# Loading two bias rows in eight one-row loads in place of five, in an adaLN attention and MLP decode kernel

## The chip, the core and the metric

The kernel runs on one core of a Trainium2 chip. The core has TensorE (PE, matmuls and their weight loads, PEld), VectorE (DVE), ScalarE (ACT), GpSimd (POOL) and SyncE (SP). SP, ACT and POOL also issue the transfers between device memory and the on-chip memory, which 16 DMA engines carry out. The metric is the device time of one execution in microseconds (us), the median of several runs. Lower is better.

## What is computed

A decode step for 8 sequences of one token each, in f32, all sizes as in the reference:

```python
x = A_x                                               # 8 x 1 x 512
mod = (silu(c) @ w_mod).reshape(8, 6, 1, 512)         # sa, ca, ga, sb, cb, gb
h = layernorm(x) * (1 + ca) + sa
# attention: 32 query heads, 8 key/value heads, head size 128, the last 2048 of 8192 cached positions
q = h @ wq
p = softmax(einsum(q, k_window) * 128 ** -0.5)
x = x + ga * (einsum(p, v_window) @ wo)
h = layernorm(x) * (1 + cb) + sb
# dense MLP with squared ReLU, inner size 1792
r = maximum(h @ w1 + b1, 0)
x = x + gb * ((r * r) @ w2 + b2)
```

The cache windows of K and V are 67 MB each; the weights wq, wo, w1, w2 and w_mod come to another 30 MB.

## The kernel before

All large inputs pass once through an on-chip tile called `home`, which is cut into four big slots of 4 MB and a small one. A list `loads` holds the order of the large transfers: w_mod, wq, then for each of 8 key/value heads two K loads and two V loads of 4 MB each, the pieces of wo in between (two of 2 MB less some rows, with the rest gathered through POOL, and two of 2 MB), and at the end the last wo piece (L146), w1 (L134, one load of 3.5 MB) and w2 (L134, four loads of 2 MB, 1 MB and twice 256 KB). `pump` issues the next load of the list on SP's queue as soon as its slot is free, and `done` frees a slot after the last reader of its contents.

The main loop (L588 on) goes over 32 quarters of K, with V five steps behind. DVE turns K around in 128 transposes (L229), PE forms the scores (L400), `soft_a` to `soft_g` do the softmax of a head in pieces between the transposes (the last of them is the transpose of the probabilities, pT, L466), and PE forms the weighted sums of V (L486). `gather` and `project_o` (L538) multiply by wo. The order of the instructions of each engine is written out by hand: the whole kernel stands in a manual schedule.

After the loop comes the tail: the attention result is brought into rows (L648 to L652), the second norm is computed (L657 to L674), the first MLP product is summed in PSUM with b1 as the first term (L679, then L688 with w1), ReLU and square follow on DVE (L695 to L700), the second product is summed with b2 as the first term (L703, then L707 with w2), and two DVE operations (L715, L716) and one store (L717, on SP's queue) end it. `spin` stands for matmuls whose result isn't used (L581).

`late_tiles` is called once, at the step after the last head's scores (`g == HKV`, `i == 1`), right after `soft_g`. It takes the buffer that held the last head's probabilities before their transpose (`pr4`), and so its writes have to wait for that transpose (L466). It clears a part of it on POOL and loads b1 (1792 values as 4 rows of 448) and b2 (512 values as 4 rows of 128) into 4 partitions each. These loads are issued by ACT (L574).

Two things about semaphores are needed to follow the steps. Every load and store that SP or ACT issues signals its landing on one of eight load semaphores, numbered 0 to 7 here, which are handed out in turn over both queues. An instruction that depends on a load waits for its semaphore, and a load itself isn't issued before the load that had the same semaphore last has landed. And after the store, SP waits for all the semaphores of the program one after the other (L749), up to two in one instruction, before the engines meet for the end.

Of the kernel before, what the change touches and what calls it, by code (L numbers as in the profile page):

```python
# [20 lines left out]
def tile_adaln_cached_attention_mlp(  # L21
# [23 lines left out]
    NQ = D // P  # L45
# [518 lines left out]
    def late_tiles():  # L564

        late = work.tile([P, NJ, 8, 4], F32, name="pr4", bufs=1).rearrange("p j x w -> p (j x w)")
        rT = late[:, : FC * 32].rearrange("p (c b) -> p c b", b=32)
        b1_in, b2_in, x1, h2T = late[:NQ, 512 : 512 + FG], late[:NQ, 1024:1152], late[:, 1152:1280], late[:, 1280:1408]
        h2T = h2T.rearrange("p (c b) -> p c b", b=32)
        nc.gpsimd.memset(rT, 0.0)  # L570
        for t, v, cuts in ((b1_in, b1, (0, 2, 3, 4)), (b2_in, b2, (0, 2, 4))):
            v = v.rearrange("(g n) -> g n", g=NQ)
            for x, y in zip(cuts, cuts[1:]):
                nc.scalar.dma_start(t[x:y], v[x:y])  # L574
        return rT, b1_in, b2_in, x1, h2T
# [12 lines left out]
    for s in range(N + PV_LAG + 1):  # L588
        g, i = divmod(s, C)
        q, h = divmod(s, 2)  # L590
        v = s - PV_LAG
# [24 lines left out]
        if i == 1 and soft:  # L616
            soft_g(g - 1)
            if g == HKV:
                spin(2)
                rT, b1_in, b2_in, x1, h2T = late_tiles()  # L620
# [133 lines left out]
```

## Time and profile before

| | |
|---|---|
| median of 3 runs | 392.83 us (392.76 to 392.84) |
| the profiled execution's own time | 392.84 us |
| its span, first to last instruction | 391.1 us |
| mean granted TensorE clock | 0.891 of full speed |
| moved by DMA | 165.04 MB, mean 422 GB/s |
| busy: PE, DVE, ACT, POOL | 68%, 57%, 12%, 3% of the span |
| SP's queue q1 | 98.0% of the 16 DMA engines' time |
| ACT's queue q10 | 80 packets, 0.04 MB |

Times in the rows are microseconds from the start of the span. In a timeline row the first number is the start, the second the duration, then engine, line, operation and tiles; a queue's name ends in q (SPq, ACTq). In the rows that count transfers, "DMA packets" gives the packets that began in a window of time and how many of them were small, and a row such as "q1 hardware_dynamic" gives one queue's packets, megabytes and the time that its packets took as a share of the window on all 16 engines; a packet whose time goes beyond a short window makes a share above 100%. A row "A <- B: t, n, m" says that A waited for B for t us in total, n times, m us the longest.

### The profile page before, as it was taken

How to read it: one execution, taken by the hardware profiler on the slowest of the kernel's cores; microseconds unless marked ns; L12 is line 12 of the kernel's file. 1: busy time of each engine (PE TensorE's matmuls, PEld its weight loads, DVE VectorE, ACT ScalarE, POOL GpSimd, SP SyncE). 2: the span in 40 equal slices, each digit the busy share in tenths (PEclk: the TensorE clock that was granted, in tenths of full speed). 3: DMA queues.
4: the chain of work that ended last, by engine and by line, in shares of the span. 5: the costliest groups of instructions: out<-in, count | busy, mean ns of one | idle time of the engine just before them, and what ended most of it. 6: DMA issues, size and time to landing. Idle time of an engine off the chain costs nothing.

```text
span 391.1 us, 4847 instructions
## 1 busy us (share of the span) xinstructions
PE 264.5 (68%) x2078; PEld 84.7 (22%) x2078; DVE 224.2 (57%) x316; ACT 46.7 (12%) x91; POOL 10.2 (3%) x36
## 2 busy tenths in 40 slices
PE   0054958878337973798289737783788237998985
PEld 0021211112011321243013212320222011334433
DVE  1054099879057935775569457381788057855232
ACT  0020011221003100310031003100201003004010
POOL 4000000000000000030000000200000000000000
PEclk9998789989859995999599959987799859999999
DMA  8999999999999999999999999999999999999995
GB/s 328 433 429 430 441 439 436 427 432 411 432 429 432 431 432 436 431 434 422 424 431 442 434 429 419 427 432 434 429 427 422 439 432 431 421 429 428 443 409 213
DMA packets 6725, 165.04 MB, mean 422 GB/s; under 512 B 968, under 2 KB 1136, under 8 KB 1392
## 3 DMA queue, kind: packets, MB, share of 16 engines
q1 hardware_dynamic: 6336, 164.17, 98.0%
q0 software_dynamic: 288, 0.53, 0.4%
q8 instruction: 16, 0.26, 0.3%
q10 hardware_dynamic: 80, 0.04, 0.0%
q14 instruction: 5, 0.04, 0.0%
HBM read 166.24 MB, written 0.07 MB: 425 GB/s over the span
## 4 chain that ended last, share of the span: by engine, by line
DMA 56%; DVE 22%; PE 16%; issue 4%; SPq 0%; ACT 0%; DVEq 0%; ACTq 0%
DMA home<-in_A_k_cache_dram 36%; DVE kT L229 12%; DMA home<-in_A_wq_dram 9%; PE s_ps L400 5%; DMA home<-in_A_v_cache_dram 5%; DMA home<-in_B_w_dram 5%; DVE pT L466 4%; PE p_ps L431 3%; PE o_ps L486 3%; PE m_ps L345 3%; DVE pr L459 2%; DVE mx L414 1%; DVE qbd L363 1%; PE m_ps L416 1%; PE m_ps L436 1%
## 5 line engine op out<-in xcount | busy, mean ns | idle before, releaser
L229 DVE STREAM_TRANSPOSE kT<-home 128x1024 f32<-128x1024 f32 x128 | 151.6, 1221 | 78.7 <-DMA home<-in_A_k_cache_dram 71.5
L400 PE MATMUL s_ps<-kT,qst 128*32 128x512 f32 x512 | 129.4, 1076 | 11.2 <-DVE kT L229 11.2
L486 PE MATMUL o_ps<-home,pT 128*32 128x256 f32 x1024 | 68.8, 390 | 9.0 <-DVE pT L466 8.6
L486 PEld LDWEIGHTS o_ps<-home,pT 128*32 128x32 f32 x1024 | 33.9, 116 | 100.4 <-issue 59.8
L416 PE MATMUL m_ps<-ident,mx 128*1 128x128 f32 x16 | 4.3, 364 | 63.7 <-DVE mx L414 63.7
L400 PEld LDWEIGHTS s_ps<-kT,qst 128*32 128x32 f32 x512 | 14.3, 114 | 29.4 <-DVE kT L229 21.1
L466 DVE STREAM_TRANSPOSE pT<-pr 128x2048 f32<-128x2048 f32 x8 | 18.2, 2279 | 1.0 <-ACT pr L449 1.0
L443 ACT ACTIVATE pr<-p_ps,nm 128x512 f32<-128x512 f32 x8 | 5.5, 688 | 103.7 <-DVE nm L440 103.7
L449 ACT ACTIVATE pr<-pr,own 128x512 f32<-128x512 f32 x16 | 17.8, 1223 | 0.3
L416 PEld LDWEIGHTS m_ps<-ident,mx 128*1 128x1 f32 x16 | 0.7, 81 | 68.9 <-DVE mx L414 68.9
L410 ACT COPY ss<-s_ps 128x512 f32<-128x512 f32 x8 | 4.7, 585 | 89.1 <-issue 61.3
L388 ACT COPY qst<-q_ps 32x128 f32<-32x128 f32 x32 | 8.2, 256 | 52.6 <-PE q_ps L377 52.4
L263 PE MATMUL m_ps<-xsum,sel 128*128 128x1 f32 x2 | 0.6, 363 | 20.2 <-DVE xsum L261 20.2
L431 PE MATMUL p_ps<-ss,perm 128*128 128x512 f32 x16 | 13.8, 960 | 0.0
L345 PE MATMUL m_ps<-home,oX 128*32 128x512 f32 x64 | 9.8, 780 | 5.3 <-DMA home<-in_A_wq_dram 5.3
L440 DVE TENSOR_SCALAR nm<-m_ps 128x1 f32<-128x1 f32 x8 | 1.3, 158 | 18.5 <-PE m_ps L436 18.5
L363 DVE COPY qbd<-m_ps 32x128 f32<-32x128 f32 x8 | 3.0, 374 | 14.4 <-PE m_ps L360 14.3
L152 POOL MEMSET home<- 128x2048 f32 x2 | 3.6, 1803 | 240.8 <-PE wo_ps L538 240.8
L503 DVE TENSOR_SCALAR o_sb<-o_ps,bit 128x128 f32<-128x128 f32 x16 | 5.2, 328 | 7.9 <-PE o_ps L486 7.7
L459 DVE TENSOR_SCALAR pr<-pr,own 128x512 f32<-128x512 f32 x16 | 9.3, 663 | 0.8 <-ACT pr L443 0.8
L581 PE MATMUL q_ps<-ident 128*128 128x512 f32 (+1 forms) x20 | 9.6, 586 | 0.0
L241 DVE TENSOR_SCALAR e_sb<-e_sb 128x128 f32<-128x128 f32 x1 | 0.2, 227 | 15.7 <-ACT e_sb L240 15.7
(133 smaller groups left out, 149.0 us busy)
## 6 DMA issues: line engine op xcount, KB each, us to landing
home<-in_A_k_cache_dram SPq DMA_DIRECT2D x16, 4096.0 KB, 27.3
home<-in_A_v_cache_dram SPq DMA_DIRECT2D x16, 4096.0 KB, 20.2
home<-in_w_mod_dram SPq DMA_DIRECT2D x1, 6144.0 KB, 17.7
home<-in_A_wo_dram SPq DMA_DIRECT2D x2, 2048.0 KB, 24.5
home<-in_A_wo_dram SPq DMA_DIRECT2D x2, 1792.0 KB
home<-in_B_w_dram SPq DMA_DIRECT2D x1, 3584.0 KB, 23.3
home<-in_B_w_dram SPq DMA_DIRECT2D x1, 2048.0 KB, 18.2
home<-in_B_w_dram SPq DMA_DIRECT2D x1, 1024.0 KB
```

The costliest lines, as they stand in the source:

```text
L229: nc.vector.transpose(KTS[q, j][:, rows], k[:, rows, 32 * j : 32 * j + 32])
L345: nc.tensor.matmul(pqs[r][32 * g : 32 * g + 32, :], hT[:, kc, :], w[:, 4 * r + g, :], start=(kc == 0), stop=(kc == NQ - 1),)
L363: nc.vector.tensor_copy(qbd[b, 4 * r : 4 * r + 4, j].rearrange("p g (b t) -> p t g b", t=REP), pT_[b].rearrange("p (t g b) -> p t g b", t= ...
L388: nc.scalar.copy(own[b, :, :, i, 0], pq[b, :P].rearrange("p (c m t) -> p c m t", c=2, t=REP))
L400: nc.tensor.matmul(s_ps[0][32 * g : 32 * g + 32, :], qst[hk % 2][:, P * (4 * c + u) + 32 * j :][:, :32], kT[:, u], start=(c == 0 and j == ...
L416: nc.tensor.matmul(MX_[hk][0:1, :P], mx, ident, start=True, stop=True)
L431: nc.tensor.matmul(sp, perm, SS_.pop(hk), start=True, stop=True)
L449: nc.scalar.mul(X_[hk][..., w], pr, own[:, w : w + 1])
L459: nc.vector.tensor_scalar(X_[hk][..., w], pr, own[:, w : w + 1], None, op0=ALU.mult)
L466: nc.vector.transpose(PT_[hk].rearrange("p e j r -> p j e r"), X_.pop(hk).rearrange("p j x w -> p j (x w)"))
L486: nc.tensor.matmul(O_[n][32 * g : 32 * g + 32, : 2 * DH], PT_[hk][:, e, j : j + 2].rearrange("p j r -> p (j r)"), vt[:, j : j + 2, :].rear ...
L581: nc.tensor.matmul(spin_ps, ident, ident[:, None, :w].to_broadcast([P, 4, w]), start=True, stop=True)
```

## The change

Each of the two bias rows is cut at every partition, so that every one of the 4 + 4 rows is a load of its own: eight loads in place of three and two. Nothing else in the program text differs. The loads are still issued by ACT in the same place and move the same bytes. Since the semaphores are handed out in turn, three more loads also move each later load of the turn, and the store, on by three places.

```diff
@@ -568,7 +568,7 @@
         b1_in, b2_in, x1, h2T = late[:NQ, 512 : 512 + FG], late[:NQ, 1024:1152], late[:, 1152:1280], late[:, 1280:1408]
         h2T = h2T.rearrange("p (c b) -> p c b", b=32)
         nc.gpsimd.memset(rT, 0.0)
-        for t, v, cuts in ((b1_in, b1, (0, 2, 3, 4)), (b2_in, b2, (0, 2, 4))):
+        for t, v, cuts in ((b1_in, b1, range(NQ + 1)), (b2_in, b2, range(NQ + 1))):
             v = v.rearrange("(g n) -> g n", g=NQ)
             for x, y in zip(cuts, cuts[1:]):
                 nc.scalar.dma_start(t[x:y], v[x:y])
```

## The prediction

> **What bounds the kernel now.** I read the page first, then the chain that ended last, then the queues of SP and ACT, then the transfers in narrow windows of time. The page says that the transfer engines never rest before the end, and that one queue, q1, which SP feeds, is nearly all of it:
>
> ```profile
> span 391.1 us, 4847 instructions
> DMA  8999999999999999999999999999999999999995
> q1 hardware_dynamic: 6336, 164.17, 98.0%
> DMA 56%; DVE 22%; PE 16%; issue 4%; SPq 0%; ACT 0%; DVEq 0%; ACTq 0%
> ```
>
> So the last byte of w2 sets the end, and a change of the order of issue costs time where a ring (one of the 16 engines' share of q1) runs out of work. The end of the chain, in order of time (start, duration), shows the place:
>
> ```profile
> 344.11 21.05 DMA home<-in_A_v_cache_dram
> 365.19 0.05 issue
> 365.24 0.33 SPq L134
> 365.67 20.29 DMA home<-in_B_w_dram
> 386.01 1.75 PE m_ps L707 x48
> 387.78 0.30 DVE y L715
> 388.10 0.29 DVE y L716
> ```
>
> The last V load lands at 365.19, w2 follows, PE takes its last pieces as they land, and two short DVE steps and the store close the program. Next, what SP and ACT issue around the bias loads (timeline rows, one row of SP's waits, one size row with the time to landing):
>
> ```profile
> 345.59 0.33 SPq L146 DMA_DIRECT2D home<-in_A_wo_dram  x1
> 355.31 0.33 SPq L134 DMA_DIRECT2D home<-in_B_w_dram  x1
> 365.24 0.33 SPq L134 DMA_DIRECT2D home<-in_B_w_dram  x1
> SPq L134 <- DMA home<-in_A_v_cache_dram: 18.8, 2, 9.5
> 357.38 1.46 ACTq L574 DMA_DIRECT2D pr<-in_B_b_dram  x5
> 374.32 0.37 ACT L649 COPY at_i<-wo_ps 128x256 f32<-128x256 f32 x1 [17.81 <-DVE at_i L648]
> home<-in_A_wo_dram SPq DMA_DIRECT2D x1, 2048.0 KB, 24.5
> ```
>
> SP is held twice, 18.8 us in all, by V loads in front of w1 (355.31) and of the first w2 piece (365.24), although neither overwrites what those V loads bring. That is the turn of the eight semaphores: a load isn't issued before the load eight places ahead of it in the turn has landed.
>
> **The turn, before and after.** Counted through the program, the last V load has semaphore 0, the bias loads 1 to 5, the last wo load 6, w1 7, the four w2 pieces 0 to 3, the store 4. Hence w1 waits for the V load before the last, the first w2 piece for the last one: the two waits above. With eight bias loads in the same place they take 1 to 7 and 0. The wo load then gets semaphore 1, w1 gets 2, the w2 pieces 3 to 6, the store 7. So the wo load waits for the first bias row, w1 for the second, the w2 pieces for the third to sixth, the store for the seventh. The bias loads can't be issued before 357.38, because their tile is free only after the last pT transpose; the wo load was issued at 345.59. This is the part of the change that costs: SP stands still with the wo load, w1 and all of w2 behind it.
>
> **When the first bias row is in.** The queue of the bias loads is q10. Its rows, for 360.6 to 362.5, for 362.5 to 362.7, for 360 to 365 and for 365 to 370:
>
> ```profile
> q10 hardware_dynamic: 3, 0.00, 0.5%
> q10 hardware_dynamic: 1, 0.00, 0.3%
> q10 hardware_dynamic: 10, 0.01, 0.5%
> q10 hardware_dynamic: 6, 0.00, 0.1%
> ```
>
> Five loads with eight rows make 16 packets, two for each row: its bytes and its semaphore write. The first load has two rows, so its four packets are the four up to 362.7: bytes, bytes, a semaphore write by 362.5, the second one between 362.5 and 362.7. The row that becomes the first load alone is done at one of these; I take the later, 362.63 within that window, because that is when the load that comes first in the queue is known to be complete. From the last semaphore packet of a transfer to SP's next issue is 0.59 (364.65 for the last V load, shown below, to 365.24). The wo load is then issued at 362.63 + 0.59 = 363.22, 17.6 us later than now.
>
> The Trainium skill, page "DMA: Bandwidth & Descriptors", section "Why a DMA increments its semaphore by 16 and not by 1", states that a copy runs on as many engines as divide its rows, the lowest-numbered ones. By that rule, which speaks against the change, all eight rows lie on the one engine that holds the single-row loads today, and the later end is the right one; with the earlier end, at 362.00, the sum would be 0.63 us smaller, 393.1. The two packets for each row agree with it; which engine takes them no row here names.
>
> **When the rings run out.** Packet counts of 362.3 to 364.1, of 364.1 to 364.7, of 362.73 to 362.76 and of 364.64 to 364.66:
>
> ```profile
> DMA packets 30, 0.59 MB, mean 329 GB/s; under 512 B 6, under 2 KB 8, under 8 KB 8
> DMA packets 31, 0.26 MB, mean 441 GB/s; under 512 B 13, under 2 KB 15, under 8 KB 15
> DMA packets 2, 0.02 MB, mean 546 GB/s; under 512 B 1, under 2 KB 1, under 8 KB 1
> DMA packets 2, 0.02 MB, mean 819 GB/s; under 512 B 1, under 2 KB 1, under 8 KB 1
> ```
>
> Packets under 512 B are semaphore writes, and one comes when a ring ends the V load. Without q10's (two and one), 4 of 16 rings end it before 364.1 and 12 from 364.1 to 364.66. Today each goes on with a 16 KB wo packet at once, as the third and fourth rows show. After the change a ring that ends before the wo load's packets exist stands idle. How long an issue takes to its first packet on idle rings, by the two such issues of the trace (the store, window 388.42 to 389.28; w_mod at the start, window 1.7 to 1.8):
>
> ```profile
> 388.42 0.35 SPq L717 DMA_DIRECT2D out_dram<-y  x1
> DMA packets 1, 0.00 MB, mean 1 GB/s; under 512 B 0, under 2 KB 1, under 8 KB 1
> 0.74 0.39 SPq L164 DMA_DIRECT2D home<-in_w_mod_dram  x1
> DMA packets 5, 0.25 MB, mean 2458 GB/s; under 512 B 0, under 2 KB 0, under 8 KB 0
> ```
>
> That is 0.85 for the store and 1.01 for w_mod: wo packets from 364.07 to 364.23, I take 364.15, the middle, as the case is a load like the one and late in the program like the other. The 12 rings that end last hardly notice. The earlier ones lose up to 1.75 us, and for a ring that is ahead of the others this is free as long as it stays ahead.
>
> One is not. The ring that ends V at 362.74 is 1.9 ahead of the last (364.65), but spends it: rows of 369.76 to 369.78, 370.82 to 370.84, and a normal w1 packet at 376.83 to 376.85, then the count of 377.4 to 378.1:
>
> ```profile
> q8 instruction: 1, 0.02, 337.8%
> q1 hardware_dynamic: 1, 0.03, 486.2%
> q1 hardware_dynamic: 1, 0.03, 332.8%
> DMA packets 32, 0.28 MB, mean 398 GB/s; under 512 B 15, under 2 KB 15, under 8 KB 15
> ```
>
> A share times its window of 0.02 us times 16 engines is a packet's time: 1.08 for the instruction packet, 1.56 for the slow w1 packet behind it, 1.065 for a normal one. The ring does eight wo packets of 0.61 from 362.75, two of w1 from 367.65 to 369.77, the instructions, the slow one at 370.83 and five more: 370.83 + 1.56 + 5 x 1.065 = 377.71. Fifteen rings end w1 within 377.4 to 378.1, the last at 378.05. So its lead has shrunk to 0.34. Idle from 362.74 to 364.15, 1.41 us, it comes in last, 1.41 - 0.34 = 1.07 us behind the time at which w1 ends now; w2 queues behind on the same ring. With the two latencies as bounds: 0.99 to 1.15. The first ring (362.41) is 1.6 ahead at the end of w1 (that is the sixteenth, which ends before 377.4), so its 1.74 stays within the pack.
>
> **What hides nothing and what does.** w1 lands 1.07 later, L688 starts 1.07 later, w2's last piece too, and the 8 matmuls, two DVE steps and the store follow it as they do now: the 1.07 is all on the path.
> - w1 and w2 on SP wait for the second to sixth row. Ten packets at one per 0.6 to 1.2 us behind 362.63 put the sixth before 375; the wo load alone keeps the rings busy for 8 x 0.61 = 4.9 us, w1 for 8.5 more, to 377.6. Nothing runs dry; if that cover were gone, each us late is a us.
> - wo landed at 345.59 + 24.5 = 370.09; some 0.3 later is before L538 needs it (371.87 below).
> - ACT issues three more loads at 1.46 / 5 = 0.29 each, 0.9 us. Two go out once their V loads, long landed, are seen; the last one waits for the last V load, 365.19. ACT has nothing to do before 374.32, so this costs nothing; without the gap it would be 365.5 - 358.8 = 6.7 us.
> - The last b2 row is needed by L703 at 381.85, 16 us after its issue; the five loads now take from 357.38 to before 370, under 13 us.
>
> ```profile
> 371.87 1.92 PE L538 MATMUL wo_ps<-home,oT 128*32 128x512 f32 x16 [0.44 <-DVE oT L527]
> 381.85 0.48 PE L703 MATMUL m_ps<-pr,qsel 4*128 4x128 f32 x2
> ```
>
> - The close. SP's waits at the end, the four that pass from the landing of the store on, and how long SP waited for it:
>
> ```profile
> L749 SPq EVENT_SEMAPHORE  x4: 28/28/28, 390.0 to 390.2; - x4
> SPq L749 <- DMA out_dram<-y: 1.0, 1, 1.0
> ```
>
> The store's own wait is the first of four that lie 0.06 apart. With the last semaphore it is the last of them: three waits less behind the landing, -0.18 us. Bounds: 0, if the closing order follows the turn too, and -0.18.
>
> **Sum.** 1.07 - 0.18 = +0.89 on the profiled execution's 392.84 (span 391.1 and 1.74 around it): 393.73. It lies 0.01 above the median of 392.83. I predict 393.7. A measurement of this kernel tells about 0.2%, 0.79 us, from no change, so the forecast is slower by a little more than that.
>
> **Rivals.**
> - *Only the close counts* (not slower). If the three extra loads take their turn elsewhere, behind the wo load for example, the wo load keeps semaphore 6 and waits for a V load that has landed before 345.59; no ring runs dry, and 0.18 is won: 392.65. Place: the issue of L146. It decides when that issue stays before about 361.8, one latency ahead of the first ring's end. For it: the turn follows the order in which the program was laid out, which the profile doesn't show. Against: five bias loads stand ahead of the wo load now, as the two V waits of SP prove. Chance 0.28.
> - *Held, but absorbed.* The wo load is late, yet the ring at 362.74 isn't burdened again, because the instruction packet goes elsewhere or the slow packet (0.49 more) doesn't recur: the loss falls to between 0 and 0.6, and the time is 392.7 to 393.2. Against: the same program fetches the same instructions. Chance 0.11.
> - *One V packet later.* The first bias row misses its place and waits for one more V packet, (365.19 - 355.31) / 8 = 1.24 us. Then every ring stands idle, the last one 0.7, and the ring at 362.74 loses 2.65 - 0.34: 392.84 + 2.31 - 0.18 = 395.0. For it: the two rows of the first load end 0.6 apart already. Against: nothing that SP does ahead of 357.38 changes. Chance 0.11.
> - *Faster by more than 0.2%* needs 0.79 us off the transfers. The close gives 0.18; a ring relieved of a few packets of q10 gains tenths at most. Chance 0.02.
>
> **Numbers.** The forecast has 0.48; its own range is 393.3 to 394.2 (latency bounds, 0.1 either way, and some tenths for refilling the rings and for the phase of the bias row). I put 0.07 of it below 393.62. Slower by over 0.2%: 0.41 + 0.11 = 0.52. Within: 0.07 + 0.28 + 0.11 = 0.46. Faster: 0.02. The range 392.6 to 394.5 leaves out the late packet, the faster case and little else.
>
> **What would show it.** In the new profile: the wo load (L146) issued near 363.2 instead of 345.59, w1 near 364.7 instead of 355.31; SP's longest waits in front of L146 on the bias loads; fewer bytes moved from 362.4 to 364.2; w1 landing some 1 us later, L688 and L707 with it; the store's wait with no waits on loads behind it. An L146 issue that stays at 345.6 makes the prediction wrong at its first step; an issue at 363 with an unchanged end of w1, at the step of the ring that has no lead left.

## The result, and the profile after

The kernel takes 394.9 us (median of 6 runs, 394.33 to 395.21), the kernel before 392.79 beside it (392.69 to 392.95): a ratio of 1.0052, with an interval of 1.0039 to 1.0065. It is slower, as forecast, but by 2.1 us where 0.9 was forecast, and it lies outside the range of 392.6 to 394.5.

The profiled execution took 395.21, 2.37 more than the one before. From its page the span, the DMA engines' busy tenths and SP's queue:

```profile
span 393.4 us, 4851 instructions
DMA  8999999999999999999999999999999999999993
q1 hardware_dynamic: 6336, 164.17, 97.5%
```

q1's share fell from 98.0 to 97.5%, and the DMA engines rest a little earlier at the end (3 in place of 5 in the last slice), so something behind the transfers has grown longer. The end of the chain (start, duration) says where both lie:

```profile
357.51 0.23 ACTq L574
...
357.79 6.55 DMA pr<-in_B_b_dram
...
364.39 16.23 DMA home<-in_B_w_dram
...
380.66 4.61 PE m_ps L688 x32
...
387.00 3.31 PE m_ps L707 x112
390.33 0.30 DVE y L715
390.66 0.29 DVE y L716
```

It now runs through a bias row of 1,792 bytes. Behind w1's landing at 380.62 it waits for no transfer any more: L688, some short DVE steps, then all 112 matmuls of L707 in one piece. Before, PE waited for w2's pieces and had 48 matmuls of L707 left when the last ones came. What SP and ACT issue, and what SP waits for (timeline rows and rows of SP's waits):

```profile
362.89 0.33 SPq L146 DMA_DIRECT2D home<-in_A_wo_dram  x1
364.39 3.43 SPq L134 DMA_DIRECT2D home<-in_B_w_dram  x5
390.98 0.35 SPq L717 DMA_DIRECT2D out_dram<-y  x1
357.51 7.81 ACTq L574 DMA_DIRECT2D pr<-in_B_b_dram  x8
SPq L146 <- DMA pr<-in_B_b_dram: 18.3, 1, 18.3
```

The wo load was issued at 362.89 (forecast 363.22), w1 at 364.39 (364.7), and the wo load waited 18.3 us for a bias row. The turn of the semaphores works as counted. The loss is in what the rings did with a load that came this late. Packets of 363.8 to 366, first after, then before:

```profile
DMA packets 54, 0.58 MB, mean 261 GB/s; under 512 B 16, under 2 KB 19, under 8 KB 19
q1 hardware_dynamic: 47, 0.57, 88.4%
```

```profile
DMA packets 71, 0.82 MB, mean 374 GB/s; under 512 B 17, under 2 KB 21, under 8 KB 21
q1 hardware_dynamic: 63, 0.82, 87.6%
```

The share of time in q1's packets is the same, but 30% less was moved in it. The packets themselves took longer. Three rows of after (windows 364.01 to 364.03, 365.52 to 365.54, and 364.3 to 364.65), then two of before (363.615 to 363.625, and 364.3 to 364.65):

```profile
q1 hardware_dynamic: 2, 0.02, 507.5%
q1 hardware_dynamic: 1, 0.02, 475.3%
q1 hardware_dynamic: 10, 0.10, 110.9%
```

```profile
q1 hardware_dynamic: 1, 0.02, 381.9%
q1 hardware_dynamic: 13, 0.11, 77.9%
```

Share times window times 16: a first wo packet at 364.02 took 1.62 us and one at 365.53 took 1.52, where a packet of the same 16 KB took 0.61 before. In the stretch in which most rings end V (the last V load), six such packets (0.10 MB) took 1.109 x 0.35 x 16 = 6.2 us, 1.04 each, against 4.36 us for seven, 0.62 each. The end of w1 carries the mark: semaphore writes of q1 (the packets under 512 B) in the windows 377.85 to 378.8 and 379.8 to 380.3,

```profile
DMA packets 34, 0.35 MB, mean 371 GB/s; under 512 B 14, under 2 KB 14, under 8 KB 14
DMA packets 13, 0.18 MB, mean 360 GB/s; under 512 B 2, under 2 KB 2, under 8 KB 2
```

so 14 rings end w1 0.4 to 0.7 later than fifteen did before (377.4 to 378.1), and two come in more than a microsecond behind them, at 379.84 and 380.23. In the trace each packet of a ring starts within 0.01 us of the end of the one before it. Followed in this way, the first of the two is the ring whose first wo packet began at 364.02, the second the one that began at 365.53, and the same two are last at the end of w2 (388.5 and 388.8). The very last semaphore write of w2 lies in the window 388.8 to 388.9 of after and 386.7 to 386.8 of before; the row is the same for both:

```profile
DMA packets 1, 0.00 MB, mean 0 GB/s; under 512 B 1, under 2 KB 1, under 8 KB 1
```

The transfers end 2.1 us later. But y (L715) starts 390.33 - 387.78 = 2.55 later, and the other 0.5 is PE's. Its first matmuls on w1, with the granted clock of two stretches (the number behind the count), after and then before:

```profile
380.66 4.55 PE L688 MATMUL m_ps<-home,pr 128*32 128x448 f32 x32 [1.85 <-DMA home<-in_B_w_dram]
378.00:380.00 2.00, 0.81 (x4) 1.00 0.94 403
380.00:382.00 2.00, 1.34 (x8) 0.50 0.99 426
382.00:384.00 2.00, 2.00 (x20) 0.65 0.96 406
```

```profile
378.70 3.21 PE L688 MATMUL m_ps<-home,pr 128*32 128x448 f32 x32 [0.25 <-DMA home<-in_B_w_dram]
380.00:382.00 2.00, 2.00 (x24) 1.00 1.07 455
```

PE stood idle for 1.85 us in front of L688 in place of 0.25, the clock was at 0.50 from 380 to 382, and the 32 matmuls took 1.34 us longer. That used up the slack PE had against w2 and 0.5 more. Last, the waits behind the store (SP's semaphore waits in the windows 391.3 to 391.8 and 392.4 to 392.7):

```profile
L749 SPq EVENT_SEMAPHORE  x6: 17/28/28, 391.4 to 391.7; - x6
L749 SPq EVENT_SEMAPHORE  x1: 28/28/28, 392.5 to 392.5; - x1
```

Six waits now pass while the store is under way and one is left at its landing, where four were. The store was issued 390.98 - 388.42 = 2.56 later and the execution took 2.37 longer, so the close gave 0.19.

### The profile page after: what moved, and what is told of

Same layout as the page of the kernel before. It is cut to its first block, busy times and chain, and to the rows that moved or that the text cites. A ratio compares the mean times of both kernels' runs of the same rounds, so it can differ in the third digit from the quotient of the medians.

```text
span 393.4 us, 4851 instructions
## 1 busy us (share of the span) xinstructions
PE 261.3 (66%) x2078; PEld 83.2 (21%) x2078; DVE 224.0 (57%) x316; ACT 46.8 (12%) x91; POOL 10.2 (3%) x36
## 3 DMA queue, kind: packets, MB, share of 16 engines
q1 hardware_dynamic: 6336, 164.17, 97.5%
## 4 chain that ended last, share of the span: by engine, by line
DMA 59%; PE 19%; DVE 18%; issue 3%; ACT 1%; SPq 0%; ACTq 0%; DVEq 0%
DMA home<-in_A_k_cache_dram 43%; DVE kT L229 11%; DMA home<-in_A_wq_dram 9%; PE s_ps L400 8%; DMA home<-in_B_w_dram 4%; PE o_ps L486 3%; DVE pT L466 2%; PE m_ps L345 2%; DMA pr<-in_B_b_dram 2%; PE p_ps L431 1%; PE m_ps L688 1%; PE m_ps L707 1%; DVE pr L459 1%; DVE qbd L363 1%; DVE mx L414 1%
## 5 line engine op out<-in xcount | busy, mean ns | idle before, releaser
L345 PE MATMUL m_ps<-home,oX 128*32 128x512 f32 x64 | 8.8, 714 | 6.4 <-DMA home<-in_A_wq_dram 6.4
L431 PE MATMUL p_ps<-ss,perm 128*128 128x512 f32 x16 | 10.5, 742 | 0.0
L521 PE MATMUL m_ps<-o_sb,pick 128*64 128x224 f32 (+2 forms) x48 | 9.0, 324 | 0.2 <-DVE o_sb L504 0.2
```

Of the source, the lines that this page charges most:

```text
L345: nc.tensor.matmul(pqs[r][32 * g : 32 * g + 32, :], hT[:, kc, :], w[:, 4 * r + g, :], start=(kc == 0), stop=(kc == NQ - 1),)
L431: nc.tensor.matmul(sp, perm, SS_.pop(hk), start=True, stop=True)
L521: nc.tensor.matmul(dest, pick[:, x].rearrange("p t u -> p (t u)"), src, start=True, stop=True)
```

## The experiments

The theory after this result: the turn makes the wo load late, and it is lateness alone, not the rows or their number, that costs; the price is that of rings that take up a new load at the last moment. Rivals: the eight small transfers themselves disturb the bulk ones; or three more loads anywhere cost time; or the loss isn't in the transfers.

**Six loads.** b1 in four rows, b2 in two loads.

```diff
-        ... ((b1_in, b1, (0, 2, 3, 4)), (b2_in, b2, (0, 2, 4))):
+        ... ((b1_in, b1, (0, 1, 2, 3, 4)), (b2_in, b2, (0, 2, 4))):
```

> b1 in four one-row loads, b2 in the two loads of before: six bias loads, so the turn moves by one place. Theory of the turn (SP holds the last wo load until the load eight places ahead of it has landed, and rings of q1 run out of work meanwhile): the wo load now waits for the V load before the last (landed 355.2), w1 for the last V load (365.2), the first w2 piece for the first bias row; each is issued while other loads still keep the rings busy, so 392.6 to 392.9, as before. Rival of the rows (one-row loads, all on one ring, and each further load cost the time): one of the three added loads, so about a third of the +2.1, 393.5.

392.54 us against 392.68, ratio 0.9998 (0.9989 to 1.0007). SP, timeline and waits:

```profile
355.19 0.33 SPq L146 DMA_DIRECT2D home<-in_A_wo_dram  x1
SPq L146 <- DMA home<-in_A_v_cache_dram: 10.9, 1, 10.9
```

The wo load waits for the V load before the last, 10 us later than before, and it costs nothing.

**Seven loads.** b2 in three loads as well.

```diff
+        ... ((b1_in, b1, (0, 1, 2, 3, 4)), (b2_in, b2, (0, 1, 2, 4))):
```

> b1 in four one-row loads, b2 in three loads (1, 1 and 2 rows): seven bias loads. Theory of the turn: the wo load waits for the last V load itself, 365.2, so it is issued only when every ring has run dry, its first packets come from 366.1 on, and each ring stands idle between 1.5 and 3.8 us: slower than with eight loads, 395.5 to 397. Rival of the rows: two of the three added loads, about 394.2, faster than with eight.

396.88 us, ratio 1.0113 (1.0098 to 1.0128): worse than eight. The wo load waits for the last V load, so every ring runs dry. SP's issue, and the packets of 364.51 to 366.05 and of 366.14 to 366.16:

```profile
365.08 0.33 SPq L146 DMA_DIRECT2D home<-in_A_wo_dram  x1
DMA packets 0, 0.00 MB, mean 0 GB/s; under 512 B 0, under 2 KB 0, under 8 KB 0
q1 hardware_dynamic: 1, 0.02, 694.4%
```

Nothing begins for 1.54 us, and one of the first packets then takes 6.944 x 0.02 x 16 = 2.22. Five, six, seven and eight loads give no change, no change, +4.2 and +2.1: what counts is which load stands eight places ahead of the wo load.

**Eight loads by columns.** Each of the two tensors in four loads of all four partitions, so no load is a single row.

```diff
+            n = v.shape[1] // 4
+            for x in range(4):
+                nc.scalar.dma_start(t[:, n * x : n * x + n], v[:, n * x : n * x + n])
```

> Eight bias loads again, but cut by columns: four loads of b1 with 4 rows of 112 values and four of b2 with 4 rows of 32 values, none of them with one row. Theory of the turn: the wo load waits for the first of the eight as in the changed kernel and is issued at 362.5 to 363.8, so 394 to 395.6. Rival of the rows: no one-row loads on a single ring, so back to 392.8.

395.95 us (394.85 to 397.34), ratio 1.0089 (1.0069 to 1.0108); wo at 363.47. The shape of the loads isn't the cause, and with 0.6 us more of lateness the median loss is larger. PE's first matmuls on w1 (here L689) were not stretched in its profiled execution, despite the idle time:

```profile
381.02 3.21 PE L689 MATMUL m_ps<-home,pr 128*32 128x448 f32 x32 [1.87 <-DMA home<-in_B_w_dram]
```

The spread of its times is taken up below.

**b2 early.** Eight one-row loads, of which b2's four go out at an earlier loop step (`s == 6`) into columns of another tile that are read no more.

```diff
+    b2_in = xc_in[:NQ, 1, :]
...
+        if s == 6:
+            for r in range(NQ):
+                nc.scalar.dma_start(b2_in[r : r + 1], b2.rearrange("(g n) -> g n", g=NQ)[r : r + 1])
```

> All eight one-row loads stay, but the four of b2 are issued early in the main loop, into a part of the input tile that nobody reads any more. Only four bias loads stand ahead of the wo load in the turn, and the store still gets the last semaphore. Theory of the turn: the wo load waits for a load that has long landed and goes out near 344.6 to 345.6, no ring runs dry, and the close wins 0.18: 392.6. Rival of the rows: eight one-row loads cost what they cost, 394.9, or half of it if only the late ones count, 393.8.

392.51 us against 392.68, ratio 0.9995 (0.9986 to 1.0004).

```profile
344.79 0.54 SPq L146 DMA_DIRECT2D home<-in_A_wo_dram  x1
```

The same eight rows cost nothing once four of them are elsewhere in the turn. It is the lowest median of all kernels run, and not to be told from the kernel before.

**Late by PE, not by a bias row.** Before, with its five loads; the slot that the last wo load fills is read once more by a small dummy matmul, and is freed only then, so the load is late without any bias row in it. The place of the matmul sets when.

```diff
-        if not last:
+        if not last and j < 2:
             done(("wo", j))
...
+    def free_late():
+        w = slot(("wo", 2), D)
+        p = ps_1.tile([P, 512], F32, name="q_ps")
+        nc.tensor.matmul(p[:, :P], ident, w[:, 0, :P], start=True, stop=True)
+        done(("wo", 2))
```

> The kernel before with its five bias loads and its turn unchanged. One small matmul (result unused) reads the small slot late, so that the last wo load can't be issued before PE has passed it, near 359.6 in place of 345.6. Theory of the dry rings (the time of the wo load's issue alone decides, through rings of q1 that have ended V by then): all rings still carry V until 362.4, so 392.6 to 393.0. Rival (SP held back at all costs, since w1 and w2 queue behind): 14 us of delay in issue, so 393.5 or more.

392.63 us against 392.63, ratio 1.0 (0.9991 to 1.0009).

> The same, with the small matmul one step later, so that the wo load is issued near 362.6, without any added bias load and without a bias load waited for. Theory of the dry rings: its first packets come near 363.6, two or three rings have run dry by then, the ring that still has to take an instruction packet among them; 0.9 us of idle time plus a slow first packet (0.5 to 1.0) less the 0.3 of lead: 393.7 to 394.6. Step of the prediction as it was sized (idle time alone): 393.3. Rival of the loads (the cost comes from eight loads or from waiting for a bias row): no eight loads here, 392.8.

395.02 us (394.35 to 395.86), ratio 1.006 (1.0046 to 1.0074). SP's issue of wo and the packets of 363.8 to 366, in the first and in the second, and for the second PE's first matmuls on w1 (here L697):

```profile
359.82 0.33 SPq L146 DMA_DIRECT2D home<-in_A_wo_dram  x1
DMA packets 77, 0.94 MB, mean 426 GB/s; under 512 B 17, under 2 KB 20, under 8 KB 20
```

```profile
362.63 0.33 SPq L146 DMA_DIRECT2D home<-in_A_wo_dram  x1
DMA packets 59, 0.69 MB, mean 313 GB/s; under 512 B 15, under 2 KB 17, under 8 KB 17
379.94 4.91 PE L697 MATMUL m_ps<-home,pr 128*32 128x448 f32 x32 [1.26 <-DMA home<-in_B_w_dram]
```

With five bias loads and no wait for any of them, an issue at 362.63 costs the whole 2.4 us, the stretched matmuls on w1 included (4.91 us). That settles the rivals on rows and on their number: lateness alone gives a loss of this size. It is made up differently, though. The last two semaphore writes of w2 (window 388 to 388.1) and the start of y (here L724):

```profile
DMA packets 2, 0.00 MB, mean 0 GB/s; under 512 B 2, under 2 KB 2, under 8 KB 2
389.95 0.29 DVE L724 TENSOR_TENSOR y<-m_ps,modC 128x128 f32<-128x128 f32 x1 [3.38 <-PE m_ps L716]
```

The transfers end about 1.3 us later than before and y starts 389.95 - 387.78 = 2.17 later, so here some 0.9 is PE's, where it was 0.5 in the changed kernel.

**Three more loads elsewhere.** Before, with the first 2 MB piece of w2 in four loads.

```diff
-            for lo, hi in ((0, 8), (8, 12), (12, 13), (13, 14)):
+            for lo, hi in ((0, 2), (2, 4), (4, 6), (6, 8), (8, 12), (12, 13), (13, 14)):
```

> The kernel before with its five bias loads; the three added loads are in w2, whose first 2 MB load is cut into four of 512 KB. The store gets the last semaphore as in the changed kernel, the wo load keeps the sixth and goes out at 345.6. Theory of the turn: no ring runs dry; the close wins up to 0.18, so 392.5 to 392.8. Rival (three more loads anywhere cost time): above 393.5.

392.62 us against 392.63, ratio 0.9999 (0.999 to 1.0008); wo stays at 345.51. The gain at the close, 0.18, is too small to be seen in the time.

**The changed kernel once more**, for what of its trace recurs.

> The changed kernel a second time, for its trace. If the excess over the predicted 1.07 us comes from how idle rings start again (first packets of the wo load later than 0.85 to 1.01 us after the issue on some rings, and longer than 0.61 each), the second trace shows such late and long first packets again, though perhaps on other rings, with 2 us or so at the end of w1. If it came from one odd event, w1 ends about 1 us later than before here and the time is near 393.7.

394.96 us. Packets of 363.8 to 366, L688, and the clock of 380 to 384:

```profile
DMA packets 56, 0.61 MB, mean 276 GB/s; under 512 B 16, under 2 KB 19, under 8 KB 19
380.30 4.58 PE L688 MATMUL m_ps<-home,pr 128*32 128x448 f32 x32 [1.86 <-DMA home<-in_B_w_dram]
380.00:382.00 2.00, 1.70 (x12) 0.50 1.03 442
382.00:384.00 2.00, 2.00 (x23) 0.73 0.91 385
```

The slow restart and the low clock recur. Of the two late rings only one does, the one that began at 364.02 in the first trace: it ends w1 at 379.80, 1.75 later than the last ring before, and L688 starts 0.36 earlier than in the first trace.

**Where lateness begins to cost.** The same dummy matmul at two more places.

> The kernel before, the wo load held by the small matmul at a third place, so that it is issued near 360.7; five bias loads, the turn unchanged. Both sizes of the theory (idle time alone, or idle time and slow first packets) say that the wo load's packets are there from 361.6, before the first ring ends V at 362.4: 392.6 to 392.8.

392.6 us, ratio 0.9999 (0.999 to 1.0008).

> The same, held one step more, the wo load issued near 361.6, its first packets due near 362.5, when at most two rings have just ended V. Idle time alone: 392.6 to 392.9. If first packets are slow because a ring has nothing queued behind its running packet (the rings are in their last or last but one V packet by then), some first wo packets take 0.8 to 1.6 in place of 0.61 although no ring stands idle for long, and the ring that still takes the instruction packet ends late: 393.0 to 394.0.

393.41 us (392.89 to 394.02), ratio 1.002 (1.0011 to 1.0029). The issues lay at 361.02 and 361.89, 0.3 later than expected. The issue of the second, and its packet of 362.95 to 362.97:

```profile
361.89 0.33 SPq L146 DMA_DIRECT2D home<-in_A_wo_dram  x1
q1 hardware_dynamic: 1, 0.02, 481.2%
```

An issue 1.3 us ahead of the first ring's end of V (362.4) is free. The one at 361.89, some 0.6 ahead (362.5 in its trace), has a first packet of 4.812 x 0.02 x 16 = 1.54 us, and 0.76 us of loss. In its trace the granted clock stays at 1.00 from 374 to 390, w2's last semaphore write comes some 0.65 later than before and y (here L724) starts at 388.37, 0.59 later: this loss is the transfers' alone. All the kernels in order of the issue in their traces, with the rate of 363.8 to 366 and the median time (the kernel before, measured beside each, took 392.63 to 392.79):

| wo load issued at, us | kernel | rate, GB/s | time, us |
|---|---|---|---|
| 344.79 | b2 early | 390 | 392.51 |
| 345.51 | three more loads in w2 | 433 | 392.62 |
| 345.59 | before | 374 | 392.79 |
| 355.19 | six loads | 397 | 392.54 |
| 359.82 | late by PE | 426 | 392.63 |
| 361.02 | late by PE | 410 | 392.6 |
| 361.89 | late by PE | 390 | 393.41 |
| 362.63 | late by PE | 313 | 395.02 |
| 362.83 | after, once more | 276 | 394.96 |
| 362.89 | after | 261 | 394.9 |
| 363.11 | after, PE kept busy (below) | 249 | 394.45 |
| 363.46 | columns, PE kept busy (below) | 166 | 395.13 |
| 363.47 | columns | 173 | 395.95 |
| 365.08 | seven loads | 3 | 396.88 |

Kernels that lose nothing have rates from 374 to 433, so the rate shows a loss only where it falls below that: 390 at 361.89 says nothing.

**PE kept busy in front of L688.** The changed kernel, and the column kernel, with dummy matmuls where PE waits for w1.

```diff
     nc.tensor.matmul(pb[:, :B], ones, ssb, start=True, stop=True)
+    spin(1)
+    spin(1, H)
```

> The kernel after, with dummy matmuls (one of full width, one of half, about 1.7 us) behind the last small matmul ahead of L688, where PE now stands idle for 1.85 us. The output is as before. Theory: that idle time is what lowered the granted clock to 0.50 and 0.65 from 380 to 384 us, which stretched L688 from 3.2 to 4.55 us and let PE end 0.5 us later behind the last piece of w2 than before. Then the clock stays at 1.00 there, L688 takes 3.2 us, the last group of L707 takes 1.7 us behind the last piece again, and the time is 394.9 - 0.5 = 394.4 us; the landings of w1 and w2 stay 2 us late. Rival: all of the loss is in the transfers; then the time stays at 394.9 us.

394.45 us (394.0 to 395.13), ratio 1.0049 (1.0036 to 1.0063). PE's rows and the clock of 380 to 382:

```profile
380.40 3.21 PE L690 MATMUL m_ps<-home,pr 128*32 128x448 f32 x32
387.83 1.68 PE L709 MATMUL m_ps<-home,pr 128*32 128x128 f32 x48 [0.47 <-DMA home<-in_B_w_dram]
380.00:382.00 2.00, 1.95 (x22) 1.00 0.96 410
```

In the trace this is plain: the clock stays at 1.00, L688's matmuls (here L690) take 3.21 again, and PE waits for w2's pieces with 48 matmuls left. The median fell by 0.45, near the 0.5 that was expected, but the two intervals overlap, so the time alone doesn't show it. The traces do: w2's last semaphore write lies in 388.55 to 388.6, 0.1 later than in the repeat (388.45 to 388.5), and yet y starts at 389.57 in place of 389.99.

> The eight column loads, with the same dummy matmuls ahead of L688. Theory: the low clock came in some executions of the column kernel alone, and its upper times (396.7 to 397.3 us) are those; its profiled one had the clock at 1.00. Then the times draw together at 394.8 to 395.6 us. Rival: its spread comes from the restart of the rings; then the times reach from 394.9 to 397.3 us as they did.

395.13 us (394.89 to 395.64), ratio 1.0066 (1.0054 to 1.0078), where the column kernel had 1.0089 (1.0069 to 1.0108) and times up to 397.34. The upper times are gone, as expected, though these two intervals overlap as well. That they came from the low clock is not shown: none of the executions with an upper time has a trace, and a low clock as long as that of after (3.4 us at 0.50, worked out in the last section) would take at most 1.7 us from PE, while the highest time lies 2.15 above the profiled 395.19.

## Why the prediction was wrong in size

- **The turn, the issue times, who waits for whom: right.** wo 0.33 and w1 0.3 earlier than forecast; six and seven loads moved the issue to 355.19 and 365.08, as the turn says.
- **The first packets on the waiting rings: right in when for the ring of the forecast, wrong in how long.** That ring was to begin at 364.15, and a packet began at 364.02. Behind it 1.62 + 6 x 0.61 leads to 369.3, where the instruction packet lies, so it is this ring. But its first packet took 1.62, not 0.61. This is the step that failed: "The ring does eight wo packets of 0.61", and "The 12 rings that end last hardly notice". A packet of 0.61 is that of a load queued long before. With the load issued 1 to 2 us ahead, wo packets took 1.04 each even in the stretch in which most rings end V, some of them on rings that had not been idle. The forecast's own row for w_mod, five packets in a window in which 16 rings should have begun, already showed that a start from nothing isn't the same on all rings; it was read as one latency.
- **The term of 1.07 measured 2.1.** For the ring of the forecast, 1.0 more for its first packet. The instruction packet came again, and a little shorter (window 369.29 to 369.31 of after):

```profile
q8 instruction: 1, 0.02, 294.1%
```

  0.94 in place of 1.08. By the forecast's own sum, 1.07 - 0.13 (earlier start) + 1.01 - 0.14 = 1.81; the ring ended w1 at 379.84, 1.79 behind the last one before (378.05). A second ring, which began only at 365.53, 2.64 behind the issue, came in last in this execution, 0.4 behind it; in the repeat it didn't. One lead was misread without effect: the ring that ends V first ends w1 at 375.8 before (a semaphore write in 375.80 to 375.83), so it was 2.2 ahead there and not 1.6.
- **"The 8 matmuls, two DVE steps and the store follow it as they do now": wrong by 0.5.** L688 was 1.34 us longer at the low clock, and so PE ended 0.5 behind what the transfers allowed. The forecast asked what hides the work around the change and not what an idle PE does to the work that follows. The trace of the kernel with PE kept busy shows the term. Its size isn't fixed: in the kernel made late by PE at 362.63 it was some 0.9.
- **The close, -0.18: right**, measured 0.19, and 0.10 in the repeat (store 390.64 - 388.42 = 2.22 later, time 2.12 longer).
- **The cover of ACT, of L538 and of L703 held.** The eighth bias row was issued at 365.09 by ACT, whose next work starts at 374.68, and none of the three is on the chain.
- **Sum:** 2.1 + 0.5 - 0.2 = 2.4 of 2.37 on the profiled execution, and 1.7 + 0.5 - 0.1 = 2.1 of 2.12 in the repeat. The rival of one V packet more gave 395.0, near the result, by a mechanism that didn't occur: the wo load was issued earlier than forecast, not later.

What stays open is why a packet that follows its load's issue closely takes up to 1.6 or 2.2 us, and why some rings begin over 2 us late. The runs show that it hangs on the time from issue to the ring's need: it costs nothing when the load is 1.3 us ahead. They don't show what the ring spends the time on. The Trainium skill, page "DMA: Bandwidth & Descriptors", section "Latency and other measured facts", states about 0.6 us to the first byte, and an access latency of the memory of 0.2 us on average and 2 us at high load. The first packet of the wo load on any ring began at 363.85 (window 363.84 to 363.86 of after), 0.96 us behind the start of the issue and 0.63 behind its end (362.89 + 0.33), near the first figure if that is counted from the end of the issue. The two first packets shown began 1.13 and 2.64 us behind the start, so it doesn't hold for every ring; the second figure would fit the spread, but no run here shows it.

## What to carry to other kernels

Where load semaphores are handed out in turn, adding or removing a small load anywhere changes whom every later load waits for; count the turn and look at the load eight places ahead of each bulk load, because five, six, seven and eight loads gave no change, no change, +4.2 and +2.1 us. A bulk load has to be queued well before the first ring runs dry (here 1.3 us was enough and 0.6 wasn't); later than that, price the restart by what slow first packets cost (here 1 us each on the ring that had no lead), not by the latency alone. And where a landing moves, price the idle time of PE in front of it too: a clock that falls there cost half a microsecond behind the transfers in one kernel here and 0.9 in another.

## What the runs showed of the hardware

- A 16 KB packet of a load issued 1 to 2.6 us earlier took up to 1.62 us in the changed kernel and 2.22 with seven loads, in place of 0.61.
- The granted clock fell to 0.50 behind an idle time of 1.85 us of PE, and of 1.26 in the kernel made late by PE at 362.63, but not behind one of 1.87 in the column kernel. From the two windows of after, the low clock lasted (2 x 0.50 + 2 x 0.35) / 0.50 = 3.4 us; the same sum for the repeat, with 0.92 from 378 to 380, gives (0.16 + 1.00 + 0.54) / 0.50 = 3.4. The Trainium skill, page "TensorE: Matmul & The Clock Gate", section "Part 1: The HAM clock gate (the "warmup" mystery)", states half clock, and a free-running window of 3.4 us that decides. The length agrees, and a free-running window would explain why equal idle times end differently, which no run here tests. That the clock falls after at least one idle window of 3.4 us doesn't agree: 1.85 and 1.26 were enough.
